# Staging tiles as contiguous rows, and no warming matmul into a bank that is still being read

## The chip, the cores and the metric

The kernel runs on one core of a Trainium2 chip. The metric is the device time of one execution in microseconds (us); three executions of the kernel before gave a median of 868.87 us. Engines are named as in the profile: PE (matrix multiply; PEld is its weight load), DVE (vector), ACT (scalar), POOL (GpSimd) and SP, the engine whose queue issues the DMA transfers.

## What is computed

Four batches of Nystrom attention, then two MLPs over the 2304 tokens. Cut to what matters:

```python
# attention, per batch and head: q_lm, k_lm are means over 18 rows, m = 32
A, Bm, C = sm(q, k_lm), sm(q_lm, k_lm), sm(q_lm, k)
Z = Bm.T / (norm1(Bm) * norm_inf(Bm) + 1e-06)
for _ in range(6):
    Z = 2 * Z - Z @ Bm @ Z
x = A @ Z @ C @ v
# first MLP, 512 -> 1536 -> 512
xn = x / rms(x) * rms_g
x = (silu(xn @ w_gate) * (xn @ w_val)) @ w_out
# second MLP, 512 -> 2048 -> 512
h = relu(x @ w_in)
out = (s * (h * h) + b) @ w_out2
```

The MLP weights arrive as 64-bit floats.

## The kernel before

One planner, `Scheduler.run` (L167), sets the order of all engines at build time. Every operation has an engine (or a choice), a cost, a key (a due time) and named buffers; the planner walks a model of time and emits the operations one after the other. At run time each engine executes its own stream in that order and waits on semaphores, which the build derives from the regions that instructions read and write.

The work before the long matmul stretch has four strands:

- **Attention of batch 0** (`attention`, L457): DVE, ACT, PE and POOL hand small tiles to each other. Scores are transposed (L825), reduced (L826), shifted (L827, POOL), exponentiated (L828, ACT), and so on to the normalised operand of the first MLP (L933 a diagonal, L938 its broadcast by PE, L944 and L948 to L950 scaling and splitting). Four 1152-column buffers of this attention lie in `far`, the right half (columns 1152 to 2303) of each of the four rows of `xbuf`; `xbuf` (L339, 128 partitions x 4 rows x 2304 columns) later holds the first MLP's output and is free until then.
- **Weight conversion** (`narrow`, L972): a 512 KB load of 64-bit weights into a staging slot (L986, L988, issued by SP), two or three passes on ACT (L1005, L1007, L1015), and a DVE pass (L1019) that puts 32-bit weights together in `rawg` or `rawo`. A store to DRAM keeps them for the later batches (L1034, L1046). Gate and value weights (the `rows` case) use the ring `st0_r`: three slots of their own (`stage`), four in the left half of `xbuf` (`st_near`, the tiles the change is about) and three in `far` once batch 0's attention is done (`st_late`).
- **Folding** (`fused`, L1081): PE multiplies `rawg` with batch data (L1091); ACT and DVE split the result (L1103, L1104, L1106).
- **First MLP** (`hidden`, L1129): 24 matmuls of 288 columns per half (L1118), ACT and DVE make the hidden values (L1135, L1137, L1141); `out_mm` accumulates the output (L1164, L1182).

Batch 1's attention begins on PE with transposes (L587) and sums (L557) that ACT or DVE evict (L591, L592, L560). Eight PSUM banks: the first MLP and the folding share `banks[4:8]`, batch 1's attention `banks[6:8]`. **Warming matmuls** (`warm`, L1392, matmul at L1395) multiply ones into `banks[7]`, the last bank, named bank_70 in the orders below; the planner puts them where its model has PE idle (L219, L220), up to its own time of 60 us.

Of the kernel before, what the change touches and what calls it, by code (L numbers as in the profile page):

```python
# [12 lines left out]
I64 = mybir.dt.int64  # L13
# [85 lines left out]
class Scheduler:  # L99
# [67 lines left out]
    def run(self, warm):  # L167
        free = dict.fromkeys(self.engines, 0.0)
        cand = {e: [] for e in self.engines}
        for o in self.ops:  # L170
            if not o.n_deps:
                for e in o.alts:
                    cand[e].append(o)
        left = len(self.ops)
        mode = "f"
        steady = False
        while left:
            best, port = None, None
            for e, ops in cand.items():
                ready = [(t, o) for o in ops if (t := self.start_of(o, e)) is not None]  # L180
                if not ready:
                    continue
                at = max(free[e], min(t for t, _ in ready))
                if best is None or at < best[0]:
                    best = (at, e, ready)
                if e in ("dve", "pool"):
                    o = min((o for t, o in ready if t <= at + self.SOON), key=lambda o: o.key)
                    if e in o.pair and (port is None or o.key < port[3] and at < port[0] + self.WAIT):
                        port = (at, e, ready, o.key)
            if best[1] in ("dve", "pool") and port and port[1] != best[1] and port[0] < best[0] + self.WAIT:  # L190
                o = min((o for t, o in best[2] if t <= best[0] + self.SOON), key=lambda o: o.key)
                if best[1] in o.pair and port[3] < o.key:
                    best = port[:3]
            at, e, ready = best
            shift = {}
            if e == "pe" and steady:
                shift = {"f": HOLD if mode == "r" else -FETCH}
            can = sorted(((o.key + shift.get(o.mode, 0.0), t, o) for t, o in ready if t <= at + self.SOON), key=lambda x: x[:2])
            if e in ("dve", "act") and at < AHEAD_TO:
                first = can[0][2]  # L200
                till = min(at + AHEAD, max(at, can[0][1]) + first.alts[e] - self.SOON)
                soon = [(o.key, t, o) for t, o in ready if at + self.SOON < t <= till and o.key < first.key - AHEAD_KEY]
                if soon:
                    can.insert(0, min(soon, key=lambda x: x[:2]))
            for _, t, o in can:
                end = max(at, t) + o.alts[e] + o.spare.get(e, 0.0)
                if all(
                    max(free[a], self.start_of(o, a)) + d + o.spare.get(a, 0.0) >= end
                    for a, d in o.alts.items() if a != e
                ):  # L210
                    break
            else:
                _, t, o = can[0]
                a = min(o.alts, key=lambda a: max(free[a], self.start_of(o, a)) + o.alts[a] + o.spare.get(a, 0.0))
                e, at = a, max(free[a], at)
                end = max(at, self.start_of(o, a)) + o.alts[a]
            if e == "pe":
                t = max(WARM0, free["pe"])
                while (t := t + WCOST * (2 if t < COLD1 else 1)) <= min(at, WARM1) - WARMS:  # L219
                    warm()  # L220
            at = max(at, self.start_of(o, e))
            if e == "pe" and o.mode:
                steady = steady or o.mode == "r"
                if steady and o.mode != mode:
                    at = max(at, free[e] + (TO_R if o.mode == "r" else TO_F))
                mode = o.mode
            end = at + o.alts[e] * (2 if e == "pe" and at < COLD1 else 1)
            for b, s in self.slots_for(o).items():
                b.slot = s
                s.held = True  # L230
                if b.ring.queue:
                    b.ring.queue.remove(b)
            o.fn(self.engines[e])
            free[e] = end if e != "sp" else end - DMA_LAG - o.slack
            if e in o.pair:
                self.ports = end
            for b in o.bufs:
                b.left -= 1
                b.end = max(b.end, end)
                if not b.left:  # L240
                    b.slot.held, b.slot.free = False, b.end
            for u in o.users:
                u.ready[e] = max(u.ready.get(e, 0.0), end)
                u.n_deps -= 1
                if not u.n_deps:
                    for a in u.alts:
                        cand[a].append(u)
            for a in o.alts:
                cand[a].remove(o)
            left -= 1  # L250
# [31 lines left out]
def tile_nystrom_attention_two_mlps(  # L282
# [23 lines left out]
    KD = DM // 128  # L306
# [4 lines left out]
    S_ = Scheduler({"pe": nc.tensor, "dve": nc.vector, "act": nc.scalar, "pool": nc.gpsimd, "sp": nc.sync})  # L311
# [13 lines left out]
    banks = [Slot(pp.tile([128, 512], F32, name=f"bank{i}")) for i in range(8)]  # L325
# [13 lines left out]
    xbuf = sb.tile([128, KD, NT], F32, name="xbuf")  # L339
# [72 lines left out]
    st_late = [Slot(far[:, :, 256 * i:256 * i + 256].bitcast(I64)) for i in range(3)]  # L412
    for x in st_late:
        x.held = True
    st_near = [Slot(xbuf[:, :, 256 * i:256 * i + 256].bitcast(I64)) for i in range(4)]
    st0_r = Ring(st_r.slots + st_near + st_late)
    row_ops = []

# [841 lines left out]
    T, t = [], 0.0  # L1260
# [65 lines left out]
    for n in range(N_T):  # L1326
        t = T[n]
# [33 lines left out]
    for i in range(NB * F2):  # L1361
        j, f = divmod(i, F2)
        t = T2[i]
# [25 lines left out]
        wo = weights(t - LEAD + 8, w_r, src, [res])  # L1389
    second_mm(T2[-1] + 8, NB - 1, F2 - 1, wo, hs)  # L1390

    def warm():  # L1392
        if banks[7].held:
            return
        nc.tensor.matmul(  # L1395
            out=banks[7].t[:, 0:256], lhsT=ones.bitcast(BF16)[:, 0:128], rhs=ones.bitcast(BF16),
            start=True, stop=True)

    with tc.manual_schedule():
        S_.run(warm)  # L1400
# [31 lines left out]
```

## Time and profile before

| | |
|---|---|
| median of 3 executions | 868.87 us (868.45 to 869.31) |
| the profiled execution | 868.52 us, of it span 866.8 us |
| PE busy | 844.8 us, 97% of the span |
| DVE / ACT / POOL busy | 657.6 / 461.5 / 129.6 us |
| mean granted PE clock | 0.992 |

The page cuts the span into 40 slices of 21.7 us. PE is at 9 tenths or more from the fourth slice to the last but one, and below that in the first three, where the granted clock dips as well. Times within the run are us from the span's start. A row of the timeline gives start, duration, engine, line, what is written from what, how many instructions, and in brackets the idle time of the engine before it with the event that ended it. The duration of a group of PE matmuls is modelled and may run a little into the next.

### The profile page before, as it was taken

What the parts mean: (1) busy time and instruction counts of PE and PEld (TensorE: products, weight loads), DVE (VectorE), ACT (ScalarE), POOL (GpSimd) and SP (SyncE); (2) the same over time, 40 slices, a digit from 0 to 9 for tenths busy, and PEclk for the clock granted to TensorE, in tenths of its full rate; (3) what the DMA queues carried; (4) which work ended last, traced back from release to release, by engine and by line L of the source; (5) the groups of instructions that cost most, each with busy time, mean ns of one, the idle gap of its engine ahead of it and who ended that gap; (6) DMA issues with size and microseconds to landing.
All of it is one profiled execution on the core that took longest, in us unless ns stands there. A gap on an engine that the chain in (4) does not pass through costs nothing.

```text
span 866.8 us, 16127 instructions
## 1 busy us (share of the span) xinstructions
PE 844.8 (97%) x6058; PEld 693.0 (80%) x6058; DVE 657.6 (76%) x1492; ACT 461.5 (53%) x969; POOL 129.6 (15%) x185
## 2 busy tenths in 40 slices
PE   8689999999999999999999999999999999999997
PEld 6468767888788887888889888888888888888896
DVE  6667898888897896789988966766676666666686
ACT  5478998744453454598844733433343334333454
POOL 0261044722671142300000000000000000000000
PEclk9799999999999999999999999999999999999999
DMA  9789987652424222388642200100010001000100
GB/s 298 218 275 342 321 250 244 196 188 75 129 86 135 98 91 94 111 280 291 217 145 66 73 0 1 50 1 0 1 50 1 0 1 32 18 1 1 40 11 25
DMA packets 66494, 96.48 MB, mean 111 GB/s; under 512 B 24176, under 2 KB 44656, under 8 KB 66416
## 3 DMA queue, kind: packets, MB, share of 16 engines
q1 hardware_dynamic: 66224, 95.18, 34.8%
q8 instruction: 48, 0.79, 0.4%
q14 instruction: 30, 0.25, 0.1%
q10 hardware_dynamic: 192, 0.26, 0.1%
HBM read 81.27 MB, written 14.16 MB: 110 GB/s over the span
## 4 chain that ended last, share of the span: by engine, by line
PE 83%; DVE 2%; ACT 1%; DMA 0%; POOL 0%; issue 0%; POOLq 0%; SPq 0%; DVEq 0%
PE bank L1208 23%; PE bank L1072 23%; PE bank L1182 15%; PE bank L1118 14%; PE bank L1091 2%; PE bank L707 1%; PE bank L898 1%; PE bank L645 1%; DMA region<-in_q_dram 0%; PE bank L938 0%; PE bank L917 0%; POOL region L827 0%; PE bank L794 0%; PE bank L620 0%; DVE region L832 0%
## 5 line engine op out<-in xcount | busy, mean ns | idle before, releaser
L1072 PE MATMUL bank<-xh,uh 128*128 128x512 f32 (+1 forms) x320 | 119.0, 372 | 0.0
L1072 PE MATMUL bank<-xh,ul 128*128 128x512 f32 (+1 forms) x320 | 118.6, 371 | 0.0
L1373 ACT ACTIVATE hbuf<-bank 128x512 f32<-128x512 f32 (+1 forms) x78 | 43.2, 553 | 141.5 <-PE bank L1072 141.4
L1072 PE MATMUL bank<-xl,uh 128*128 128x512 f32 (+1 forms) x320 | 117.5, 367 | 0.0
L1208 PE MATMUL bank<-wh,hh 128*128 128x512 f32 x288 | 114.2, 397 | 0.3 <-DVE hh L967 0.3
L1208 PE MATMUL bank<-wl,hh 128*128 128x512 f32 x288 | 113.8, 395 | 0.0
L1208 PE MATMUL bank<-wh,hl 128*128 128x512 f32 x288 | 113.6, 394 | 0.0
L1182 PE MATMUL bank<-hh,wh 128*128 128x512 f32 (+1 forms) x224 | 87.0, 388 | 0.0
L1182 PE MATMUL bank<-hh,wl 128*128 128x512 f32 (+1 forms) x224 | 83.1, 371 | 0.0
L1182 PE MATMUL bank<-hl,wh 128*128 128x512 f32 (+1 forms) x224 | 82.8, 370 | 0.0
L968 DVE TENSOR_TENSOR hl<-hbuf,hh 128x512 fp32r<-128x512 f32 (+8 forms) x125 | 69.3, 559 | 2.8 <-ACT hh L966 0.3
L1072 PEld LDWEIGHTS bank<-xl,uh 128*128 128x128 f32 x320 | 60.2, 188 | 12.3
L1072 PEld LDWEIGHTS bank<-xh,uh 128*128 128x128 f32 x320 | 60.0, 188 | 11.5
L1072 PEld LDWEIGHTS bank<-xh,ul 128*128 128x128 f32 x320 | 60.1, 188 | 11.3
L966 ACT ACTIVATE wh<-region 128x512 fp32r<-128x512 f32 x51 | 32.2, 632 | 69.1 <-PE bank L1208 67.9
L967 DVE CAST uh<-region 128x512 fp32r<-128x512 f32 x57 | 24.3, 426 | 54.1 <-PE bank L1072 54.0
L1208 PEld LDWEIGHTS bank<-wh,hl 128*128 128x128 f32 x288 | 54.3, 189 | 13.2 <-DVE hl L968 0.2
L968 DVE TENSOR_TENSOR wl<-region,wh 128x512 fp32r<-128x512 f32 x70 | 48.4, 692 | 20.0 <-ACT wh L966 19.4
L1208 PEld LDWEIGHTS bank<-wh,hh 128*128 128x128 f32 x288 | 54.1, 188 | 11.8 <-DVE hh L967 0.7
L1208 PEld LDWEIGHTS bank<-wl,hh 128*128 128x128 f32 x288 | 54.4, 189 | 11.1
L1118 PE MATMUL bank<-xh,uh 128*128 128x288 f32 x200 | 60.6, 303 | 0.7 <-DVE hbuf L1137 0.7
L1118 PE MATMUL bank<-xl,uh 128*128 128x288 f32 x200 | 59.0, 295 | 0.0
(226 smaller groups left out, 1961.4 us busy)
## 6 DMA issues: line engine op xcount, KB each, us to landing
rawg<-keptg SPq DMA_DIRECT2D x36, 512.0 KB, 4.5
stage<-in_moe_w_out_dram SPq DMA_DIRECT2D x28, 512.0 KB, 4.5
rawo<-kepto SPq DMA_DIRECT2D x48, 256.0 KB, 2.7
stage<-in_moe_w_in_dram SPq DMA_DIRECT2D x16, 512.0 KB, 4.9
keptg<-rawg SPq DMA_DIRECT2D x12, 512.0 KB, 4.3
xbuf<-in_moe_w_val_dram SPq DMA_DIRECT2D x10, 512.0 KB, 7.5
xbuf<-in_moe_w_gate_dram SPq DMA_DIRECT2D x9, 512.0 KB, 6.9
region<-in_v_dram SPq DMA_DIRECT2D x16, 256.0 KB, 4.6
```

The costliest lines, as they stand in the source:

```text
L645: nc.tensor.matmul(out=ps.t[p, pn * g:pn * g + n], lhsT=lhsT(p, g), rhs=rhs(p, g), start=True, stop=True)
L707: nc.tensor.matmul(out=ps.t[:, 0:HC], lhsT=part(u, "bd")[:, 128 * e:128 * e + 128], rhs=part(y, "t").rearrange("p (t e i) -> p t e i", e=2 ...
L898: nc.tensor.matmul(out=pX2[i].t[:, 0:HC], lhsT=WBD.t[p, 128 * g:128 * g + 128], rhs=AT[hf, g].t[p, 0:HC], start=True, stop=True)
L966: e.activation(out=hi(), in_=src(), func=ACTF.Copy) if e is nc.scalar
L967: else e.tensor_copy(out=hi(), in_=src())), r=r, w=[wh], pair=True)
L968: b = op({"dve": t_dve(n), "pool": t_pool(n)}, key, lambda e: e.tensor_tensor(out=lo(), in0=src(), in1=hi().bitcast(F32), op=ALU.subtract) ...
L1072: nc.tensor.matmul(out=ps.t[:, 0:n], lhsT=w[a].t[:, ks], rhs=x[y].t[:, kd, 0:n], start=(kd == 0 and i == 0), stop=(kd == KD - 1 and i == 2))
L1091: nc.tensor.matmul(out=pU[g].t[m, 256 * j:256 * j + 256], lhsT=gw[b].t[p, m], rhs=r.t[p, :, 128 * k:128 * k + 128], start=True, stop=True)
L1118: nc.tensor.matmul(out=ps.t[:, 0:HC], lhsT=u[a].t[:, 256 * g + 128 * part:256 * g + 128 * part + 128], rhs=x[y].t.rearrange("p k n -> p (k ...
L1182: nc.tensor.matmul(out=A[c].t[:, 0:n], lhsT=w[a].t[:, 128 * c:128 * c + 128], rhs=hs[y].t[:, 0:n], start=(f == 0 and i == 0), stop=(f == F ...
L1208: nc.tensor.matmul(out=A[c].t, lhsT=hs[a].t[:, s], rhs=w[y].t, start=(f == 0 and i == 0), stop=(f == F2 - 1 and i == 2))
L1373: e.activation(out=r.t[:, 0:n], in_=ps.t[:, 0:n], func=ACTF.Relu) if e is nc.scalar
```

## The change

The four `st_near` slots cover the same 1024 columns of the same four rows as before. Slot i was 256 columns of every row; now it is the first 1024 columns of row i. The data of a load, its size and its source are the same. `warm` now gets the planner's time and does nothing where the last user of the bank ends later than that.

```diff
@@ Scheduler.run
                 while (t := t + WCOST * (2 if t < COLD1 else 1)) <= min(at, WARM1) - WARMS:
-                    warm()
+                    warm(t)
@@ tile_nystrom_attention_two_mlps
-    st_near = [Slot(xbuf[:, :, 256 * i:256 * i + 256].bitcast(I64)) for i in range(4)]
+    st_near = [Slot(xbuf[:, i, 0:1024].bitcast(I64)) for i in range(KD)]
@@ 
-    def warm():
-        if banks[7].held:
+    def warm(t):
+        if banks[7].held or banks[7].free + S_.CROSS > t:
             return
```

The order of the instructions is unchanged on DVE, ACT, POOL and SP; on PE 19 of the 122 warming matmuls go, in four places (3, 9, 3 and 4 of them), and nothing else moves. What changes beside is the semaphores that instructions wait for. A name such as DVE or DMAHW7 is the semaphore of an engine or of one of the DMA's completion counters.

DVE, in the middle of batch 0's attention (L825 transposes scores into the buffers in `far`, L690 is a step of the matrix iteration):

```order
 L677 TENSOR_TENSOR region<-bank_68,region 128x2x32 [waits PE_49,Activation_49]
-L825 STREAM_TRANSPOSE xbuf<-bank_65 128x288 [waits DMAHW7_49,DMAHW6_49,DMAHW5_49]
+L825 STREAM_TRANSPOSE xbuf<-bank_65 128x288
 L825 STREAM_TRANSPOSE region<-bank_66 128x288
 L690 SCALAR_TENSOR_TENSOR region<-region,bank_69 128x128 [waits DVE_49,PE_49,Activation_49]
 L826 TENSOR_REDUCE region<-xbuf 128x9 [waits DVE_49]
 L826 TENSOR_REDUCE region<-region 128x9 [waits DVE_49]
-L825 STREAM_TRANSPOSE xbuf<-bank_67 128x288 [waits DMAHW0_49]
+L825 STREAM_TRANSPOSE xbuf<-bank_67 128x288
 L690 SCALAR_TENSOR_TENSOR region<-region,bank_68 128x128 [waits DVE_49,PE_49]
```

The rows stand where they stood; the two transposes into `xbuf` no longer wait for four DMA loads. The same four waits go from a PE transpose (L772), a POOL subtraction (L827) and an ACT exponential (L828).

SP, the loads of gate and value weights in the same stretch (the first four `xbuf` rows are the four `st_near` slots):

```order
 L988 DMA stage_93<-in_moe_w_gate_dram 128x4x128 [waits DMAHW4_49]
-L988 DMA xbuf<-in_moe_w_val_dram 128x4x128 [waits DMAHW5_49,DVE_49,Activation_49]
+L988 DMA xbuf<-in_moe_w_val_dram 128x4x128 [waits DMAHW5_49]
 L988 DMA xbuf<-in_moe_w_gate_dram 128x4x128 [waits DMAHW6_49]
 L988 DMA xbuf<-in_moe_w_val_dram 128x4x128 [waits DMAHW7_49]
-L988 DMA xbuf<-in_moe_w_gate_dram 128x4x128 [waits DMAHW0_49,DVE_49]
+L988 DMA xbuf<-in_moe_w_gate_dram 128x4x128 [waits DMAHW0_49]
 L988 DMA stage_91<-in_moe_w_val_dram 128x4x128 [waits DMAHW1_49,Activation_49]
```

The fourth of these loads no longer waits for DVE; the loads and their order are the same.

PE, between the first half of unit 0 of the first MLP (L1118) and batch 1's transposes (L587); the other eight warming matmuls are left out:

```order
 L1118 MATMUL bank_67<-xl_84,uh_98 128x288
 L1118 MATMUL bank_67<-xh_82,ul_100 128x288
-L1395 LDWEIGHTS ones
-L1395 MATMUL bank_70<-ones 128x256 [waits DVE_49]
...
-L587 MATMUL bank_69<-ident,region 128x128 [waits DMAHW2_49]
+L587 MATMUL bank_69<-ident,region 128x128 [waits DMAHW2_49,DVE_49]
 L587 MATMUL bank_69<-ident,region 128x128 x2
-L587 MATMUL bank_70<-ident,region 128x128 [waits DMAHW4_49]
+L587 MATMUL bank_70<-ident,region 128x128 [waits DMAHW4_49,DVE_49]
 L587 MATMUL bank_70<-ident,region 128x128 x2
```

Nine warming matmuls go, and the transposes behind them take over the wait for DVE. Further on, three go between two groups of L587 and the next L1091, and four ahead of the L1091 after that; earlier, three of fifteen go between the second group of L917 (row sums) and L938.

## Rows read from the trace of the kernel before

**Rows 1.** Busy time of the engines, from part 1 of the page.

```profile
PE 844.8 (97%) x6058; PEld 693.0 (80%) x6058; DVE 657.6 (76%) x1492; ACT 461.5 (53%) x969; POOL 129.6 (15%) x185
```

**Rows 2.** Windows of 10 us: length, busy us of five engines, PE clock, DMA share, GB/s.

```profile
20.00:30.00 10.00, 2.87 (x76) 1.99 (x76) 2.70 (x10) 2.70 (x6) 0.93 (x2) 0.66 0.65 204
30.00:40.00 10.00, 9.85 (x179) 6.39 (x178) 8.81 (x31) 6.41 (x17) 3.72 (x6) 0.82 0.71 229
40.00:50.00 10.00, 9.25 (x75) 6.89 (x74) 7.85 (x22) 7.53 (x19) 0.00 (x0) 0.83 0.93 263
50.00:60.00 10.00, 7.09 (x65) 5.39 (x64) 5.57 (x12) 8.18 (x16) 8.49 (x12) 1.00 0.85 283
60.00:70.00 10.00, 9.05 (x87) 7.72 (x87) 8.13 (x19) 9.13 (x20) 7.24 (x10) 1.00 0.94 338
```

**Rows 3.** Timeline 15 to 50 us, all engines (columns as told above): the stall.

```profile
21.88 0.63 ACT L1005 ACTIVATE ca<-stage 128x512 f32<-128x512 f32 x1
23.96 0.48 DVE L825 STREAM_TRANSPOSE xbuf<-bank 128x288 f32<-128x288 f32 x1 [4.16 <-DMA xbuf<-in_moe_w_val_dram]
...
25.37 0.37 SPq L988 DMA_DIRECT2D xbuf<-in_moe_w_gate_dram  x1
...
28.97 0.48 DVE L825 STREAM_TRANSPOSE xbuf<-bank 128x288 f32<-128x288 f32 x1 [3.27 <-DMA xbuf<-in_moe_w_gate_dram]
...
28.99 1.12 PE L772 MATMUL bank<-ident,xbuf 128*128 128x128 f32 x4 [3.30 <-DMA xbuf<-in_moe_w_gate_dram]
...
29.77 0.44 ACT L828 ACTIVATE xbuf<-xbuf 128x288 f32<-128x288 f32 x1 [7.26 <-POOL xbuf L827]
```

**Rows 4.** Timeline 15 to 50 us: warming matmuls ahead of L938.

```profile
43.67 3.30 PE L1395 MATMUL bank<-ones 128*128 128x256 bf16 x15 [0.22 <-DVE ul L1106]
...
44.87 0.45 DVE L933 TENSOR_TENSOR region<-ident,region 96x288 f32<-96x288 f32 x1
...
46.76 0.86 PE L938 MATMUL bank<-xbuf,ones 96*128 96x288 f32 x2
...
47.66 1.18 DVE L944 TENSOR_TENSOR region<-region,bank 128x288 f32<-128x288 f32 x3 [1.75 <-PE bank L938]
```

**Rows 5.** Timeline 50 to 62 us: warming matmuls ahead of L587 and L1091.

```profile
53.94 0.45 DVE L1141 SCALAR_TENSOR_TENSOR hbuf<-hbuf,bank 128x288 f32<-128x288 f32 x1
...
54.45 1.14 PE L1395 MATMUL bank<-ones 128*128 128x256 bf16 x9 [1.64 <-DVE hbuf L1141]
...
55.43 0.82 PE L587 MATMUL bank<-ident,region 128*128 128x128 f32 x6
...
56.01 0.45 DVE L1141 SCALAR_TENSOR_TENSOR hbuf<-hbuf,bank 128x288 f32<-128x288 f32 x1
...
57.47 0.85 ACT L591 ACTIVATE region<-bank 128x384 f32<-128x384 f32 x2
...
57.99 0.49 PE L1395 MATMUL bank<-ones 128*128 128x256 bf16 x3 [0.94 <-ACT region L591]
...
58.41 0.66 PE L1091 MATMUL bank<-rawg,gw 64*32 64x256 f32 x16
...
59.16 0.38 ACT L1103 ACTIVATE uh<-bank 128x256 fp32r<-128x256 f32 x1 [0.84 <-PE bank L1091]
...
60.80 0.68 DVE L1019 SCALAR_TENSOR_TENSOR rawg<-ca,cmag 128x512 int32<-128x512 int32 x1
```

**Rows 6.** A window of 2 us, columns as in rows 2.

```profile
42.00:44.00 2.00, 1.66 (x27) 1.04 (x27) 1.81 (x6) 1.57 (x4) 0.00 (x0) 0.94 1.10 251
```

**Rows 7.** DMA issues of 0:60 (line, engine, count, KB each, median us to landing).

```profile
xbuf<-in_moe_w_val_dram SPq DMA_DIRECT2D x5, 512.0 KB, 7.7
...
stage<-in_moe_w_gate_dram SPq DMA_DIRECT2D x3, 512.0 KB, 5.2
```

**Rows 8.** SP's queue, timeline 0 to 200 us, the load of the second output weights.

```profile
63.37 0.34 SPq L986 DMA_DIRECT2D stage<-in_moe_w_out_dram  x1
```

**Rows 9.** ACT, timeline 60 to 110 us, the first pass over that load.

```profile
70.34 0.68 ACT L1005 ACTIVATE ca<-stage 128x512 f32<-128x512 f32 x1
```

## The prediction

> **What bounds the kernel now.** I read the page first: PE is busy 844.8 of 866.8 us [rows 1], and its 40 slices show that nearly all the idle time lies in the first three, before 65 us. After that PE is the bound, so a change of the early part is worth what it moves the moment at which PE's dense stretch begins, and a change of anything later would have to make matmuls cheaper. Next the 10 us windows [rows 2]: from 20 to 30 us PE is busy 2.87 us, DVE 2.70 and ACT 2.70, so here no engine is the bound; DMA is at 0.65. From 50 to 60 PE has 7.09 of 10 and ACT 8.18. From 60 to 70 PE has 9.05 and ACT 9.13: both are nearly full, and the dense stretch has begun. Last the timeline of the holes. At 19.8 us DVE stops for 4.16 us ahead of a transpose (L825) and at 25.7 for 3.27 us ahead of another; each is ended by the landing of a weight load into `xbuf`. PE waits 3.30 us for the same landing, and ACT 7.26 us for POOL, which waits for it too [rows 3]. None of these instructions uses a weight. They write buffers in the right half of `xbuf`'s rows; the loads fill the left half. A slot of 256 columns in each of four rows reaches from the first column of row 0 into row 3, and the waits are those of two regions that overlap. The fourth load is issued only at 25.37, behind DVE's own read, so it is held up by the stall and then prolongs it [rows 3].
>
> **The stall.** The order shows that with rows as slots these waits go on DVE, PE, POOL, ACT and SP. What is late next? ACT: its last free instruction ahead of the stall, L1005, ends at 21.88 + 0.63 = 22.51, and the next one, L828, began at 29.77 [rows 3]. The few DVE transposes and reductions and the one POOL subtraction that L828's operand needs fit between 19.8 and 22.5, so L828 can begin when ACT is free: 29.77 - 22.51 = **7.3 us** earlier. DVE gives the same from its side, 4.16 + 3.27 = 7.4 [rows 3]. From there to 43 us the chain runs through ACT and DVE, which are nearly full (DVE 8.81 of 10 from 30 to 40 [rows 2]), so I carry 7.3 on unchanged. PE's clock is low for part of it (0.66 and 0.82 as means [rows 2], so 6.8 + 3.6 = 10.4 us at 1.2 GHz, which fell when PE stood still); with the hole gone the small matmuls there may run at 2.4 GHz. I give that nothing, since ACT's conversions lie between, and 0.5 as the upper end.
>
> **Warming matmuls ahead of L938.** Fifteen of them begin at 43.67 and take 3.30 us, 0.22 each. The diagonals that L938 reads are ready at 44.87 + 0.45 = 45.32, but L938 stands behind the warming and starts at 46.76; DVE's L944 loses 1.75 us on it [rows 4]. Three of the fifteen go: 3 x 0.22 = 0.66 if the clock is as it was. If the clock is at 2.4 GHz, where nine take 1.14 [rows 5], twelve take some 1.5 and end at 45.2, and L938 starts when its operand is there, 46.76 - 45.32 = 1.44 earlier. The lower end is 0.66, the upper the 1.75 for which DVE waited. I take **0.9**, nearer to the lower, because the clock fell in the window of 42 to 44 us while PE was busy 1.66 of 2 us [rows 6], so the fall did not come from the stall alone.
>
> **Warming matmuls ahead of L587 and L1091.** Nine of them wait at 54.45 for DVE's read of the last bank (L1141, 53.94 + 0.45 = 54.39) and keep the transposes L587 back until 55.43 [rows 5]. L587 itself now carries that wait and starts at 54.45: 0.98 earlier. Three more wait at 57.99 for ACT's L591 and keep back L1091, which starts at 58.41. Without them it waits for the second L1141, 56.01 + 0.45 = 56.46, so it starts 1.9 earlier. ACT's L1103 behind it (59.16) still stands behind the pair L591, which ends at 57.47 + 0.85 = 58.32 and moves up by at most 0.98 to 57.34: 1.8 earlier. The last four wait for ACT too, but the L1091 behind them waits for L1019, which ends at 60.80 + 0.68 = 61.48 [rows 5] and moves with ACT; they cost nothing. The ends are 0.98 (only the first hold goes) and 1.9; I take **1.6**, because ACT has conversions between these instructions.
>
> **What the loads themselves do.** Source, size and order are the same. A load into an `xbuf` slot landed in 7.7 us, one of the same matrix kind into a contiguous `stage` slot in 5.2 [rows 7]; the shape may thus be worth anything from 0 to 2.5 us per load, most likely 0, since the `xbuf` loads ran in the fuller stretches. It is hidden either way: ACT reads them long after. What must follow the earlier PE is the supply. The tightest case that I found is the second load of output weights, issued at 63.37 and read by ACT at 70.34 [rows 8, 9]; at an ordinary landing time of about 5 us it has some 2 us to spare. It is issued when ACT frees the slot, so it moves with ACT. DMA had idle time that goes with the stall: 3.5 + 2.9 + 0.7 + 1.5 = 8.6 us in the four windows from 20 to 60 [rows 2].
>
> **The sum.** 7.3 + 0.9 + 1.6 = 9.8 us earlier at the start of the dense stretch, and PE carries it to the end. The profiled execution took 868.52 us (span 866.8 and 1.7 around it): 858.7. The median of the three runs is 0.35 higher, so I predict **859.0 us**. Lower end of the cost: 7.4 + 0.5 + 1.75 + 1.9 = 11.6, 857.3; least gain without a rival: 7.3 + 0.66 + 0.98 = 8.9, 860.0.
>
> **Rivals.** *The clock falls.* Sixteen of the nineteen matmuls kept PE at work between 52 and 62 us; without them it has little to do there beside L587 and L1091, and the clock may drop to 1.2 GHz as the dense stretch begins. A low stretch costs half its length there. The trace has one of 10.4 us in rows 2 and one of about 3.4 (40 to 50 us at 0.83, so 10 x 2 x 0.17): 1.7 to 5.2 us given back, gain 8.1 to 4.6, **860.8 to 864.3**. For it: the clock did fall at the end of a busy window [rows 6]. Against it: it stayed at 1.00 from 50 to 60 [rows 2], and the longest hole that rows 5 show there is 1.64 us, which was there before too; by the working above the change leaves one more, ahead of the L1091 that waits for L1019, of about that length. The Trainium skill (TensorE: Matmul & The Clock Gate, section HAM oscillation) puts such falls down to idle gaps between bursts of matmuls. By that alone, with holes this short, the sum would stay at 859.0; the trace does not quite agree, with a fall in a window in which PE was busy 1.66 of 2.00 us [rows 6], so the rival keeps its chance.
>
> *DMA becomes the bound.* From 60 us on DMA is at 0.94 [rows 2]. If the supply cannot come 9.8 us earlier, the gain is at most the 8.6 us of idle time that DMA gets back, and at worst half of it: **860.3 to 864.6**. Against it: ACT, not a landing, set the pace of the conversions.
>
> *The stall stays.* If something else holds DVE at 19.8 us for as long, for instance the landing of data that it does need, only 0.9 + 1.6 remain: **866.4**. Against it: the order shows no other DMA wait there.
>
> *Slower.* The clock drops while PE is short of work and does not come back within the dense stretch. Half of the low time is lost, so from 2 x 9.8 = 19.6 us of low clock on the kernel is slower: 30 us would give 859.0 + 15 = **874**. Against it: each low stretch of the trace ended within some 10 us, and with less work on PE than the dense stretch gives.
>
> **How the numbers follow.** Forecast 0.63 (857.3 to 860.0), clock 0.20, DMA 0.11, stall stays 0.03, slower 0.03. The range begins a little below the lower end, at 856.8, since a clock that stays high would also shorten L938 itself, and reaches to 863.2. Above that lie about a third of the clock's and of the DMA's cases and the last two: 0.06 + 0.04 + 0.06 = 0.16. A difference of 0.2%, 1.7 us, is about what a measurement of this kernel can tell from none. Forecast, clock and DMA are faster by more than that, 0.94; the stall's 2.5 us is close to it, so of its 0.03 I put 0.01 under faster and 0.02 under same. Faster 0.95, same 0.02, slower 0.03.
>
> **What would show it.** In the profile after, DVE and ACT have no wait for a load between 19 and 30 us, L828 starts near 22.5 and L938 near 38.6 (46.76 - 7.3 - 0.9). The second L1091 of batch 0, at 58.41 before, starts between 48.3 and 49, and PE's dense stretch (61.48 before) near 51.7. From there each row should stand 9.8 us earlier to the end; if the lead shrinks on the way, the row where it shrinks names the rival: PEclk below 1.00 is the clock, ACT or DVE waiting for a landing is DMA. I am wrong if L828 starts later than 24, or if PE has new idle time after 52 us.

## The result

The changed kernel took 860.84 us, the median of four executions (856.92 to 861.46); the kernel before took 868.98 beside it. The ratio is 0.9897, 95% interval 0.9868 to 0.9927: faster by 1.0%. That is 1.8 us more than the 859.0 that was forecast, and inside the range of 856.8 to 863.2. The four were 861.0, 861.46 and 860.67 with a mean granted clock of 0.994, and 856.92 with 0.999; the profiled one is the 861.0 (span 859.3 us). So what follows explains the 861 that three of four took; the execution of 856.92 left no trace.

First, the stall. The timeline of 19 to 30 us, with the columns of [rows 3]:

```profile
19.65 0.47 DVE L825 STREAM_TRANSPOSE xbuf<-bank 128x288 f32<-128x288 f32 x1
...
21.16 0.67 POOL L827 TENSOR_TENSOR xbuf<-xbuf,region 128x288 f32<-128x288 f32 x1 [2.64 <-DVE region L826]
21.35 0.47 DVE L825 STREAM_TRANSPOSE xbuf<-bank 128x288 f32<-128x288 f32 x1
...
22.36 0.43 ACT L828 ACTIVATE xbuf<-xbuf 128x288 f32<-128x288 f32 x1
...
24.16 0.26 PE L645 MATMUL bank<-region 32*32 32x32 f32 x8
26.95 0.33 PE L645 MATMUL bank<-region 32*32 32x32 f32 x8 [2.53 <-issue]
27.34 0.22 ACT L698 ACTIVATE region<-bank 128x64 f32<-128x64 f32 x1 [1.85 <-PE bank L645]
```

The two transposes into `xbuf` stood at 23.96 and 28.97 behind a landing [rows 3]; now they have no wait, and ACT's L828 begins at 22.36 instead of 29.77, 7.41 us earlier (7.3 was expected). Between 19 and 30 us no engine waits for a load any more.

The two PE rows above show something that the prediction did not have. In the middle of a group of sixteen small matmuls, after eight of them, PE stands still for 2.53 us. "issue" means that it waited for nothing the profile shows. The list of DMA queues by window (packets, MB, share of the engines' time) shows what came in that moment. The changed kernel, 22 to 24 and then 24 to 26 us:

```profile
q1 hardware_dynamic: 702, 0.69, 110.0%
...
q1 hardware_dynamic: 621, 0.70, 107.0%
q8 instruction: 1, 0.02, 3.6%
```

The kernel before, 22 to 24 us:

```profile
q1 hardware_dynamic: 173, 0.16, 24.2%
q8 instruction: 1, 0.02, 3.5%
```

q8 carries instructions: one packet of 16 KB here. Its 0.77 MB over the span come to about 64 bytes for each of PE's 6039 matmuls and 6039 weight loads, so it is taken to be PE's own queue. Before, the packet started at 22.42 us, when the data of the early loads was running out and every engine stood in the stall, and PE came to this group only at 32.78; its cost was nil. In the changed kernel the DMA engines are full without a break from 20 to 34 us (shares of 1.02 to 1.11 in the windows below), because the loads no longer wait for the attention: the fourth into `xbuf` is issued at 17.71 us instead of 25.37. The packet starts at 24.31. The Trainium skill (Runtime: NRT & Kernel Launch, section Instruction fetch mechanics) says that the sequencer fetches its program in 16 KiB blocks through a DMA queue of its own, and that crossing a block's boundary is "mostly hidden". The trace agrees with the block's size (47 packets of q8, 0.77 MB over the span); here, behind full DMA engines, the crossing was not hidden.

Second, the clock. Windows of 2 us of the changed kernel, columns as in [rows 2]:

```profile
22.00:24.00 2.00, 1.61 (x59) 1.12 (x60) 1.83 (x10) 2.00 (x7) 0.46 (x1) 1.00 1.10 347
24.00:26.00 2.00, 0.42 (x16) 0.23 (x17) 1.86 (x7) 1.46 (x3) 1.34 (x2) 1.00 1.11 356
26.00:28.00 2.00, 1.05 (x15) 0.51 (x16) 0.17 (x1) 0.64 (x3) 0.67 (x1) 0.51 1.05 404
28.00:30.00 2.00, 2.00 (x37) 1.22 (x36) 1.04 (x4) 1.40 (x2) 0.00 (x0) 0.50 1.02 410
30.00:32.00 2.00, 2.00 (x31) 1.17 (x24) 1.48 (x6) 0.00 (x0) 1.19 (x2) 0.50 1.02 409
32.00:34.00 2.00, 2.00 (x28) 1.20 (x27) 1.79 (x7) 0.00 (x0) 0.15 (x1) 0.78 1.11 344
```

PE had stood still since 24.4 us when the granted clock fell to 0.50, that is 1.2 GHz, at about 26, and it stayed there to about 33. Four warming matmuls then take 1.03 us instead of 0.61, and they stand between the steps of the matrix iteration that everything waits for. The changed kernel, and then the kernel before:

```profile
28.55 1.03 PE L1395 MATMUL bank<-ones 128*128 128x256 bf16 x4
```

```profile
33.28 0.22 ACT L698 ACTIVATE region<-bank 128x64 f32<-128x64 f32 x1
...
34.10 0.61 PE L1395 MATMUL bank<-ones 128*128 128x256 bf16 x4
...
38.71 2.53 ACT L904 ACTIVATE region<-bank 128x288 f32<-128x288 f32 x8 [3.36 <-PE bank L898]
```

L828's lead of 7.41 us is down to 5.94 at L698, which reads what the halved L645 writes (33.28 before, 27.34 now), and to 4.11 when ACT reads the next product (L904, 38.71 before, 34.60 now). So the hole and the slow clock cost **3.3 us**: 1.5 up to L698, behind the hole, and 1.8 after it, in the stretch at the low clock.

Third, the warming matmuls. The timeline of 34 to 56 us:

```profile
34.60 2.53 ACT L904 ACTIVATE region<-bank 128x288 f32<-128x288 f32 x8 [5.20 <-PE bank L898]
...
39.57 2.63 PE L1395 MATMUL bank<-ones 128*128 128x256 bf16 x12 [0.22 <-DVE ul L1106]
...
41.99 1.17 PE L938 MATMUL bank<-xbuf,ones 96*128 96x288 f32 x2
...
43.20 1.18 DVE L944 TENSOR_TENSOR region<-region,bank 128x288 f32<-128x288 f32 x3 [1.38 <-PE bank L938]
...
44.86 0.38 PE L1118 MATMUL bank<-xh,uh 128*128 128x288 f32 x1
...
48.93 0.44 DVE L1137 SCALAR_TENSOR_TENSOR hbuf<-hbuf,bank 128x288 f32<-128x288 f32 x1
49.43 1.10 PE L587 MATMUL bank<-ident,region 128*128 128x128 f32 x6 [1.08 <-DVE hbuf L1137]
...
51.50 1.22 PE L1091 MATMUL bank<-rawg,gw 64*32 64x256 f32 x16
...
52.80 0.38 ACT L1103 ACTIVATE uh<-bank 128x256 fp32r<-128x256 f32 x1
...
53.78 0.99 PE L1091 MATMUL bank<-rawg,gw 64*32 64x256 f32 x16 [0.21 <-DVE ul L1106]
54.44 0.68 DVE L1019 SCALAR_TENSOR_TENSOR rawg<-ca,cmag 128x512 int32<-128x512 int32 x1
```

Two rows of the kernel before that [rows 4, 5] do not have:

```profile
49.29 0.38 PE L1118 MATMUL bank<-xh,uh 128*128 128x288 f32 x1
...
68.64 0.66 PE L1091 MATMUL bank<-rawg,gw 64*32 64x256 f32 x16
```

Row by row, the lead is 4.77 us at L938 (46.76 before), 4.43 at the first L1118 (the two L938 ran at the low clock, 1.17 us instead of 0.86), 6.00 at L587, 6.91 and 7.70 at the two L1091, and 7.39 at the next one (68.64 before, 61.25 now). From there it stays: the span is 7.5 us shorter. The windows of 10 us show PE busy 9.30 from 50 to 60 us (7.09 before) and 10.00 from 60 to 70 (9.05), with the clock at 1.00 in both: no new idle time there.

### The profile page after: what moved, and what is told of

The parts are those of the page before. It is cut to its first block, busy times and chain, and to the rows that moved or that the text cites. A ratio compares the mean times of both kernels' runs of the same rounds, so it can differ in the third digit from the quotient of the medians.

```text
span 859.3 us, 16086 instructions
## 1 busy us (share of the span) xinstructions
PE 843.6 (98%) x6039; PEld 691.4 (80%) x6039; DVE 658.2 (77%) x1492; ACT 460.6 (54%) x969; POOL 130.0 (15%) x185
## 4 chain that ended last, share of the span: by engine, by line
PE 90%; DVE 4%; ACT 3%; issue 1%; DMA 0%; POOL 0%; DVEq 0%; ACTq 0%; POOLq 0%
PE bank L1208 23%; PE bank L1072 23%; PE bank L1118 17%; PE bank L1182 16%; PE bank L1091 3%; PE bank L1164 2%; PE bank L707 1%; PE bank L898 1%; PE bank L645 1%; PE bank L1395 1%; PE bank L938 1%; ACT cmag L1007 0%; DMA region<-in_k_dram 0%; PE bank L720 0%; PE bank L794 0%
## 5 line engine op out<-in xcount | busy, mean ns | idle before, releaser
L1208 PEld LDWEIGHTS bank<-wl,hh 128*128 128x128 f32 x288 | 54.4, 189 | 11.1
L1118 PE MATMUL bank<-xh,uh 128*128 128x288 f32 x200 | 60.7, 303 | 0.7 <-DVE hbuf L1137 0.7
L1118 PE MATMUL bank<-xl,uh 128*128 128x288 f32 x200 | 59.0, 295 | 0.0
```

Of the source, the lines that this page charges most:

```text
L1118: nc.tensor.matmul(out=ps.t[:, 0:HC], lhsT=u[a].t[:, 256 * g + 128 * part:256 * g + 128 * part + 128], rhs=x[y].t.rearrange("p k n -> p (k ...
L1208: nc.tensor.matmul(out=A[c].t, lhsT=hs[a].t[:, s], rhs=w[y].t, start=(f == 0 and i == 0), stop=(f == F2 - 1 and i == 2))
```

## The experiments

All are compared with the kernel before (868.65 to 868.98 in these runs) and, by their traces, with the changed kernel.

**The rows alone.** The slots of the change, with the warming of the kernel before:

```diff
-    st_near = [Slot(xbuf[:, :, 256 * i:256 * i + 256].bitcast(I64)) for i in range(4)]
+    st_near = [Slot(xbuf[:, i, 0:1024].bitcast(I64)) for i in range(KD)]
```

> The kernel before with the four staging slots as rows, and all 122 warming matmuls left in. My theory of the sum: the stall at 19.8 us goes (7.3 us), and PE then stands still for its own instructions at about 24 us, whose transfer waits behind a DMA that no longer has a hole there, and loses 3 to 4 us with the clock that falls on it; the part of the warming matmuls (0.7 us before L938, 1.6 to 3 us before L587 and L1091) stays lost. So about 863 to 865 us in most executions, L828 near 22.4. Rival (the missing warming matmuls let the clock fall, and that is what cost the 3 us): with all of them in, the low clock between 26 and 33 us is not there, and the time is about 869 - 7.4 = 861.5 in every execution.

Measured 861.97 us (859.94 to 863.42), ratio 0.9922 (0.9900 to 0.9945). L828 stands at 22.46, so the stall is worth its 7.3 us. Its trace has the hole too, at the same matmul:

```profile
26.79 0.33 PE L645 MATMUL bank<-region 32*32 32x32 f32 x8 [2.27 <-issue]
```

All 122 warming matmuls are in this kernel, so the hole comes with the rows and not with the missing warming. The time is below what was expected and is the number that the rival gave, but not for its reason: the low clock is there, at 0.68 and 0.50 in 26 to 30 us. It ended at 30 us, and the fifteen warming matmuls ahead of L938 ran at the upper level, in 1.80 us. With all warming matmuls in place the lead is the same 7.0 us at the first L1118 (42.28) and at the second of the two L1091 (54.46), so what the change gains between these rows is the warming rule's. The four executions took 859.94, 861.23, 862.71 and 863.42 us at mean clocks of 1.000, 0.998, 0.996 and 0.994: the time goes with the clock.

**The warming rule alone.** The slots as before, `warm(t)` as in the change.

> The kernel before with the nineteen warming matmuls left out and the staging slots as they were. By the prediction's sum: 0.9 + 1.6 = 2.5 us, about 866.4. By the trace of the changed kernel, where L938 gained 0.7 on what came before and the stretch from L1118 to the third L1091 another 3.0: 865.3. If the nineteen matmuls had been holding the clock up (rival), the clock is low for some us between 52 and 62 and the gain is under 1 us or none, 868 to 869.

Measured 866.52 us (864.72 to 867.24 in ten executions), ratio 0.9972 (0.9962 to 0.9982): 2.2 us. The granted clock is 1.00 from 50 us on, so the dense stretch does not need the nineteen. In the profiled execution L828 is 0.57 us later than before and the second of the two L1091 2.97 us earlier (58.51): the rule gains some 3.5 us between them, and the 2.2 are what is left after that late start and later rows.

**Two loads moved back.** The changed kernel, with the value weights of unit 2 and the gate weights of unit 3 (issued at 16.39 and 17.71 us) issued behind the load that waits for ACT at 22 us. The one line of the edit, shortened to its condition:

```diff
+    lambda e: pend.append(lambda: load(e))        # (kind, f, part) in ((1, 2, 1), (1, 3, 0))
+    lambda e: (load(e), [p() for p in pend])      # (kind, f, part) == (1, 3, 1)
```

> The changed kernel with two of its eight early weight loads (the value weights of unit 2 and the gate weights of unit 3) issued behind the load that waits for ACT at 22 us instead of at 16.4 and 17.7 us; all else in the same order. Theory (PE's instructions wait behind a full DMA): DMA runs dry near 20 to 21 us as it did before the change, the transfer of PE's instructions starts by 22.5 instead of 24.3, PE has no hole of 2.5 us at 24.4, the clock stays up through 26 to 33 us, and all executions take about 857, as the fastest of the changed kernel did (856.9). Rival (the hole has another cause, such as ACT or DVE being late): the hole stays and the time is 860 to 861.

Measured 857.49 us (857.13 to 859.40), ratio 0.9879 (0.9857 to 0.9901). The median is 3.35 us below the change's; the intervals overlap, since one of the change's four executions was at 856.92. The four kernels of this study with a load moved back and with warming after 20 us (this one and three below) bear it out: of their sixteen executions fifteen took 856.2 to 857.7, and of the twelve executions of the change and of the two kernels described next only one did. The DMA queues at 20 to 22 us, and PE's next steps:

```profile
q1 hardware_dynamic: 414, 0.41, 61.3%
q8 instruction: 1, 0.02, 3.5%
```

```profile
24.33 0.33 PE L645 MATMUL bank<-region 32*32 32x32 f32 x16
...
25.58 0.22 ACT L698 ACTIVATE region<-bank 128x64 f32<-128x64 f32 x1
...
25.86 0.43 PE L645 MATMUL bank<-region 32*32 32x64 f32 x16 [0.76 <-ACT region L698]
...
30.82 2.53 ACT L904 ACTIVATE region<-bank 128x288 f32<-128x288 f32 x8 [3.17 <-PE bank L898]
```

The packet starts just before 22.0 us, the sixteen matmuls are whole, the clock stays at 1.00 until after 34 us, and L904 stands at 30.82, 7.9 us before its old place. From L698 to L904 it takes 5.24 us at this clock, and 7.26 in the change. Nothing was taken out of the kernel; two loads that nobody needs yet were issued later.

**Another shape of slot.** The changed kernel, each slot still within one row, as four pieces of 256 columns with gaps of 32:

```diff
-    st_near = [Slot(xbuf[:, i, 0:1024].bitcast(I64)) for i in range(KD)]
+    st_near = [Slot(xbuf[:, i, 0:1152].rearrange("p (k c) -> p k c", k=KD)[:, :, 0:256].bitcast(I64)) for i in range(KD)]
```

> The changed kernel with each staging slot still within one row, but as four pieces of 256 columns with a gap of 32 between them instead of 1024 columns in one piece. Theory (the gain is from slots that no longer reach over other rows): the waits are those of the changed kernel, and so is the time, 857 to 861.5. Rival (the gain, or a part, is from loads that land in one piece in each partition): the loads land later, by up to 2.5 us each, and some of the 8 us is lost again, 863 or more.

Measured 860.36 us (858.29 to 860.58), ratio 0.9900 (0.9881 to 0.9919), the time of the change. The gain comes from the regions not overlapping, not from the contiguous destination. The landings differ little: median 8.1 and 7.9 us (value and gate weights into `xbuf`, up to 60 us), 7.5 and 7.7 in the change, 7.7 and 7.8 before. The hole is there, 1.69 us long.

**One load more behind.** The changed kernel with an extra load of 512 KB right behind the last early one. The call that the edit adds, without the line around it:

```diff
+    e.dma_start(out=hbuf[:, 0:1024].bitcast(I64).rearrange("p (k f) -> p k f", k=KD), in_=wt[:, c].rearrange("(k p) f -> p k f", p=128))
```

> The changed kernel with one more load of 512 KB, into a buffer that nothing uses yet, right behind the eighth early weight load (the data is not used). Theory (PE's instructions wait behind the data that is queued ahead of them): the transfer of PE's instructions starts some 1 to 1.5 us later than the 24.3 of the changed kernel, PE's hole grows from 2.5 to about 4 us, at the same instruction, and the time is 861 to 863. Rival (the hole has nothing to do with how much is queued): hole 2.5 us and time 860.8 as before.

Measured 859.88 us (858.35 to 861.38), ratio 0.9893 (0.9876 to 0.9910). This missed: the hole did not grow.

```profile
18.60 1.69 SPq L998 DMA_DIRECT2D hbuf<-in_moe_w_gate_dram  x1
...
27.03 0.33 PE L645 MATMUL bank<-region 32*32 32x32 f32 x8 [2.52 <-issue]
```

The extra load is issued at 18.60 us, and the packet starts at 24.47 us, against 24.31 in the change. So it is not the fullness of the DMA engines alone that decides; the data of a load issued at 18.60 did not stand ahead of the instructions.

**No warming ahead of L938.** The kernel with the two loads moved back, less the twelve warming matmuls ahead of L938 (`or 35.7 < t < 38` added to the condition in `warm`).

> The kernel with the two deferred loads, and without the twelve warming matmuls that stand ahead of L938. Theory: L938 starts when its diagonal is ready, near 37.1 instead of 38.3, since the warming at a low clock took 2.7 us there; DVE and ACT follow, and the time is about 1.2 us lower, 856.3. Rival (the warming brings the clock back in time for L1118): the clock stays low for longer, L938 and the first L1118 run at half speed, and the 1.2 us are lost again or more, 857.5 to 859.

Measured 856.82 us (856.20 to 857.47), ratio 0.9858 (0.9843 to 0.9872). L938 starts when its operand is there, at 36.96 instead of 38.30, and the clock falls behind it instead of ahead (thirteen warming matmuls at 38.14 take 2.98 us). Half of the 1.34 us is left in the medians (0.67); the intervals of the ratios overlap.

**No warming after 20 us.** The kernel with the two loads moved back, `or t > 20` in the condition.

> The kernel with the two deferred loads and no warming matmul at all after 20 us (54 pairs fewer than there). It measures what the warming is worth, and whether a clock that falls without it was the danger that the prediction named. Theory: the clock falls near 25 us and stays low until the dense stretch of L1118, some 15 to 20 us at 1.2 GHz; the chain there runs on DVE and ACT, so it loses 1 to 2 us on the small matmuls and up to 1.7 us when the dense stretch begins at a low clock: 858 to 861. Rival (the warming only holds the matmuls behind it): 855 to 857.

Measured 858.00 us (857.39 to 858.83), ratio 0.9874 (0.9858 to 0.9891). The clock was low in 27.8 to 34.6 and 38.0 to 44.9 us, and still the ratio is that of the kernel with 54 more warming matmuls (0.9879; the medians are 0.5 us apart). As far as this pair of runs tells, what these matmuls win by the clock they nearly lose again by standing in the way.

**Ten matmuls fewer at 15 us.** The changed kernel without ten warming matmuls near 15 us, which are twenty instructions of PE (`or 15 < t < 16.25`).

> The changed kernel without ten of the warming matmuls near 15 us, twenty PE instructions ahead of the hole. Theory (PE stops where the instructions that it has end, whatever they are): the hole moves on by twenty instructions; all sixteen matmuls of the L645 that was cut in two run, two of the three warming matmuls behind it too, and the hole lies there; ACT's L698 then has its input in time, the chain loses about 1 us instead of 2.5, and the time is 858 to 860. Rival (PE stops because of what the L645 needs): the hole stays between the two halves of that L645.

Measured 857.88 us (856.55 to 860.04; 856.55, 860.04, 856.69 and 859.07), ratio 0.9872 (0.9852 to 0.9892). PE's rows:

```profile
24.25 0.33 PE L645 MATMUL bank<-region 32*32 32x32 f32 x16
24.51 0.39 PE L1395 MATMUL bank<-ones 128*128 128x256 bf16 x2
26.76 0.27 PE L1395 MATMUL bank<-ones 128*128 128x256 bf16 x1 [1.85 <-issue]
26.95 0.43 PE L645 MATMUL bank<-region 32*32 32x64 f32 x16
```

The hole has moved on by eight matmuls and two warming ones, each with its weight load: twenty instructions, exactly as many as were taken out ahead. Counted in the traces, 346 matmuls and 347 weight loads stand ahead of the point where PE goes on, in all six kernels with a hole. PE stops where the instructions that it has end. The profiled execution is the 856.55, with the clock at 1.00; the two slower ones had mean clocks of 0.994 and 0.996 and left no trace.

**One load moved back.** As with two, but only the gate weights of unit 3 (issued at 17.71 us).

> The changed kernel with only one early load moved behind the load that waits for ACT at 22 us: the gate weights of unit 3, issued at 17.71 us in the changed kernel. (With the value weights of unit 2, issued at 16.39, moved as well, PE's hole was gone: 857.49.) Theory A: PE's instructions are held up by all the data that is ahead of them in the DMA engines when they are asked for; 512 KB less, some 1.5 us at 350 GB/s, then brings them 1 to 1.5 us earlier: the 16 KB lie in 22 to 24 us instead of 24 to 26, PE's hole shrinks from 2.53 us to about 1.0 to 1.5, and the median is about 859. Theory B: they pass or stand ahead of the last load already, as they did ahead of the extra load that was issued at 18.60: the hole stays at 2.2 to 2.6 us and the median at 860 to 861. Theory C: all that counts is whether the DMA engines are full at the moment: with one load less they run dry before 24 us, and the hole goes altogether, about 857.5.

Measured 857.53 us (856.77 to 857.70), ratio 0.9870 (0.9854 to 0.9887). The DMA queues at 22 to 24 us, and PE's hole:

```profile
q1 hardware_dynamic: 353, 0.35, 66.9%
q8 instruction: 1, 0.02, 3.5%
```

```profile
25.38 0.26 PE L645 MATMUL bank<-region 32*32 32x32 f32 x8 [0.70 <-issue]
```

The packet starts earlier than in the change and later than with two loads moved, and the hole is 0.70 us, between 2.53 and none. That is nearest to theory A, with a smaller hole than the 1.0 to 1.5 that it gave; the time is the one that theory C gave, though the hole did not go altogether. It is that of two loads moved: the clock was low in 26 to 30 us, but was at 1.00 at L938, where it was low with two moved. Windows of 0.02 us place the start of the packet in every kernel:

| kernel | q8 packet starts at | PE goes on at | hole |
|---|---|---|---|
| two loads moved back | 22.00 us | no stop | none |
| the same, no warming ahead of L938 | 22.05 | no stop | none |
| one load moved back | 22.96 | 25.38 | 0.70 |
| slots in four pieces | 23.82 | 26.27 | 1.69 |
| ten matmuls fewer | 24.29 | 26.76 | 1.85 |
| the change | 24.31 | 26.95 | 2.53 |
| rows alone | 24.36 | 26.79 | 2.27 |
| one load more | 24.47 | 27.03 | 2.52 |

In the six kernels with a hole, PE goes on 2.42 to 2.64 us after the packet starts, wherever that is.

**Both edits.** The kernel without the twelve ahead of L938, less the ten at 15 us as well.

> The best version so far (two early loads moved back, and no warming matmuls ahead of L938: 856.82) without ten warming matmuls near 15 us as well. Theory: PE's instructions arrive at 22 us anyway with the two loads moved, so the ten matmuls of margin buy nothing there, and the clock is at its upper level in both: 856.8, no difference. Rival: the run without the ten (and with the loads in their old places) kept the clock at 1.00 to 60 us and reached 856.55 in its profile; if it is the ten matmuls that keep the clock up by moving PE's work, this kernel has no low stretch before 60 us either and takes 855.0 to 856.0.

Measured 856.48 us (856.37 to 856.83), ratio 0.9861 (0.9846 to 0.9876), no difference from 856.82. The rival falls: its windows from 36 to 44 us have a clock of 0.50 and 0.71, so the ten matmuls are not what kept the clock up. The two kernels of about 856.5 have the lowest medians of the study. Both beat the kernel before. Against the change their medians are 4.0 and 4.4 us lower, but the intervals of the ratios still touch (0.9872 and 0.9876 against 0.9868).

## Why the prediction was right, and where it was not

**The stall** was worth what the sum said: 7.4 us by L828, against 7.3. The reading behind it (false waits of two overlapping regions, and ACT late next, when L1005 ends) holds, and the run with pieces within one row shows that the overlap is the cause.

**"From there to 43 us ... I carry 7.3 on unchanged"** is the step that failed. It took as next bound ACT and DVE, both seen in the trace of before, and never asked whether PE would have its instructions. The packet was in that trace, one line in the window of 22 to 24 us, hidden by the very stall that the change removes. The hole and the clock that fell behind it cost 3.3 us on the way to L904. The run with two loads moved back has no hole and no fall there, keeps L828's lead up to L904, and its span is 3.6 us shorter than the change's (855.7 against 859.3): about the same number by another way. The rival that DMA becomes the bound was near it in its cause and wrong in its form: no data came late.

**The clock rival** (1.7 to 5.2 us given back) named a cost that came, in the wrong place. The clock was to fall after 52 us for want of warming matmuls; there it stayed at 1.00, with the rule alone as in the change. It fell at 26 us, behind the hole, and took 1.8 us up to L904 and another 0.3 at L938, where it fell again as it had before. By the prediction's own sign, a lead that shrinks where PEclk is below 1.00, these rows point to the clock; for the hole ahead of them the prediction had no sign.

**The term of L938**, 0.9 with a lower end of 0.66, measured 0.66 (4.77 less the 4.11 at L904). Three matmuls fewer at the low clock, and no more. Its other case is on record too: with ten matmuls fewer near 15 us the clock was at 1.00 there, the twelve took 1.47 us, and the lead grew by 1.76 between L904 (31.92) and L938 (38.21).

**The term of L587 and L1091**, 1.6, was mis-sized. The first L1118 leads by 4.43 us and the rows of L1091 in the steady part by 7.39, so it measured 3.0. Its three parts: L587 gained 1.57 instead of 0.98, since its wait is for L1137, one instruction ahead of the L1141 for which the warming waited. ACT's L1103 gained 0.36 more, 1.93 together, where 1.8 was expected. And the last four warming matmuls, which "cost nothing" because the L1091 behind them was taken to wait for L1019, cost 1.3 us: in the new rows that L1019 starts at 54.44, after the L1091 at 53.78, which waits only for L1106. The two times stood side by side in [rows 5] (L1019 ended at 61.48, L1091 began at 61.48) by accident, and were read as a cause. Some 0.3 us of it is lost again by 61 us.

So the sum of the terms was nearer 7.4 + 0.7 + 3.0 = 11.1 us than 9.8, and 3.3 of it was taken back on the way to L904 and 0.3 at L938, with 7.5 left at the end of the span. The run with two loads moved back shows the terms without the loss: its second L1091 of the pair stands at 49.91, 11.6 us before its old place, and its span is 11.1 us shorter. The forecast came close by luck: a missing cost and a term too small by half offset each other. What the prediction named as the signs of failure, L828 after 24 us or new idle time after 52, were both absent: they did not cover idle time on PE between 24 and 27.

## What to carry to other kernels

A stall hides whatever else was due in it, so ask of every queue, that of the instructions too, what crossed the DMA engines in those microseconds, and whether it still has room once the stall is gone. Loads that nobody needs for long are best not issued in a burst ahead of a stretch of short dependent work; moving one such load back was worth as much here as moving two (857.53 and 857.49 us). And where two rows meet to the hundredth of a microsecond, look up the wait itself before calling one the cause of the other.

## What the runs showed of the hardware

PE can run out of instructions while all its operands are ready: the profile has it as a wait for "issue", in the middle of a group, after the same number of PE's instructions in six kernels, and it was over 2.4 to 2.6 us after a q8 packet of 16 KB had started. The hole was 0.70 to 2.53 us. With one and with two loads of 512 KB less ahead of it the packet started 1.4 and 2.3 us earlier (22.96 and 22.00 against 24.31 us); a load issued at 18.60 us delayed it by no more than 0.2 (24.47). How the instruction queue takes its turn among the data queues was not tried further and is open.

Nor does the length of such a hole say alone whether the clock falls: behind the hole of 0.70 us (one load moved back) it was 0.50 in the window of 26 to 28 us, and around that of 1.85 us (ten matmuls fewer) it stayed at 1.00 in every window from 20 to 60. In the kernels with both loads moved back and warming it stayed at 1.00 from 20 to 34 us. What tells these apart stays open, and so does how much of the 3.3 us would be left in an execution with the hole and without the fall.
